# New durations in the planning clock of an S4D and MLP kernel, and outer products behind instead of ahead of x1

## The chip, the cores and the metric

The kernel runs on 1 core of a Trainium2 chip. The metric is the device time of one execution in microseconds, the median of several runs; less is better.

## What is computed

A layer norm of the input feeds two branches, and their product is added to the input. One branch is an S4D convolution: a kernel K made from exponentials of 128 modes for each of 576 channels, convolved with the sequence of 2048 steps by a Fourier transform. The other is an MLP with 4608 hidden units.

```
x  = A_u                                            # 1 x 2048 x 576
xn = layernorm(x)
P  = exp((A * dt)[:, :, None] * pos);  K = 2 * einsum("dn,dnl->dl", C, P).real
s  = irfft(rfft(xn_t, 2L) * rfft(K, 2L))[:L] + xn * D_skip
h  = gelu(layernorm(xn) @ w1 + b1);  g = silu(h @ w2 + b2)
out = x + s * g
```

## The kernel before

**The MLP.** All products are made with operands split into a high and a low part. The 2048 tokens are worked in two halves of 1024, each in two blocks of 512 (`tb`), and the 4608 hidden units in 12 groups of 384. One group with one block is a slot, 48 in all. A slot has 11 positions on TensorE: three of layer 1 (L617, 14 products of 512 columns each, into `mxa` and `mxb`) and eight of layer 2 (L680, products of 288 columns). For each product of layer 1 a chain follows it: Gelu on ScalarE (L653), its high part `hh` on ScalarE (L656), its low part `hl` on VectorE (L659); layer 2 needs `hh` and `hl`. After layer 2, VectorE adds the result to `acc` (L690). VectorE and ScalarE also split the raw weights (L567, L570).

**The scan.** The S4D branch is cut into 6 chunks of 96 channels, and its tables into 36 blocks of 16 channels. For each block, VectorE and ScalarE make tables of sines and magnitudes (L914 to L956), and TensorE makes K from them by outer products, `kgen` (L995). Each chunk then has on TensorE two steps x1 (L1099), two k1 (L1130), four s2 (L1160), two inverses (L1202) and one i1 (L1228). They write into two conversion banks, both called `cv`; VectorE or ScalarE empties them: transpositions after x1 and k1 (L1107, L1138), products and sums after s2 (L1175, L1181, L1182), transpositions between the two inverse stages (L1213). At the end the branches are combined (L727, L728), and the last rows are finished by L763 to L780. The row statistics of the later tokens (L407) are made during the first slots.

**The order.** Every engine's queue is written in the order in which a planner, `Order`, traces the steps. It keeps a virtual time for each engine. Each step carries an engine and a duration, which is what the text calls its booking; `dve(n)`, `act(n)` and `pool(n)` give durations from a number of columns. A step's results are ready after its booked duration and `LAT`, 0.2 us. TensorE's MLP positions are the backbone: `unit` takes them in turn, and `advance` then traces everything on other engines that can begin before TensorE's virtual time. The chains behind layer 1 and layer 2 are `urgent`, and each of their steps has a due time, `by`, worked out from TensorE's positions still to come (`hidden_by`, `add_by`). Other steps wait in `lines`; one is traced only if it ends before the due time of the next urgent step on its engine. TensorE's own scan steps are taken between MLP positions (`pe_turns`) if they were ready 0.4 us before, and x1, k1 and s2 are spread by a timetable (`pace`). `ride` lets a block of outer products join a host step x1, k1, s2 or i1: the block's function is put into `GUEST`, and the host calls `lead` with its own conversion bank. The start of the program, before the first slot, is written out by hand.

ScalarE keeps one table of functions at a time; `self.tbl` is the virtual clock's idea of it, and a change is booked at 1.28 us. Steps with `tbl=None`, copies and squares, run with any table.

Of the kernel before, what the change touches and what calls it, by code (L numbers as in the profile page):

```python
# [19 lines left out]
NT = 16  # L20
# [15 lines left out]
TB = 512  # L36
# [3 lines left out]
def dve(n):  # L40
    return 0.075 + 0.00104 * n


def act(n):
    return 0.06 + 0.00098 * n
# [6 lines left out]
class Order:  # L52
# [85 lines left out]
    def advance(self, horizon):  # L138
        while True:
            best = None  # L140
            soon = dict(self.next)
            for u in self.urgent:
                st = u[1][0]
                k = (max(u[0], self.t[st["eng"]]), 0)
                if u[0] <= horizon and (best is None or k < best[0]):
                    best = (k, u, None)
                for st in u[1]:
                    soon[st["eng"]] = min(soon.get(st["eng"], 1e9), st["by"])
            for x in self.lines:
                if x["steps"] and x["steps"][0]["by"] < 1e9:  # L150
                    st = x["steps"][0]
                    soon[st["eng"]] = min(soon.get(st["eng"], 1e9), max(st["by"], self.t[st["eng"]] + st["dur"]))
            for n, x in enumerate(self.lines):
                h = self.head(x)
                if h is None or h[0]["eng"] == "PE":
                    continue
                st, r = h
                if st["eng"] is None:
                    k = (max(r, 0), 1 + n)
                    if r > horizon:  # L160
                        continue
                else:
                    e = st["eng"]
                    b = max(self.t[e], r)
                    d = st["dur"]
                    if st["tbl"]:
                        d += 1.28 * (1 + (st["tbl"] != self.tbl))
                    if b > horizon or b + d > soon.get(e, 1e9) + st["late"]:
                        continue
                    k = (b, 1 + n)  # L170
                if best is None or k < best[0]:
                    best = (k, None, x)
            if best is None:
                break
            if best[1] is not None:
                self.go(best[1])
            else:
                self.run(best[2])
            self.pin()
# [26 lines left out]
def step(eng, dur, fn, need=(), mark=None, cv=0, at=0.0, late=0.0, tbl=None, by=1e9):  # L206
    return dict(eng=eng, dur=dur, fn=fn, need=tuple(need), mark=mark, cv=cv, at=at, late=late, tbl=tbl, by=by)
# [3 lines left out]
def mixer_kernel(ctx, tc, u, log_a_real, a_imag, c_real, c_imag, log_dt, d_skip, w1, b1, w2, b2,  # L211
                 f1, f2, g2, g1, tvals, ident, out, parts=("mlp", "s4d")):
    nc = tc.nc
# [145 lines left out]
    A2 = sb.tile([P, 16, 2, CH, 2], F32, name="A2")  # L359
# [617 lines left out]
    def lead(q):  # L977

        if GUEST:
            GUEST.pop()(q)  # L980
# [46 lines left out]
    def chunk(c):  # L1027
# [57 lines left out]
        def x1(i):  # L1085
            Q = {}
            in_parts("x", i, lambda: XC[i].rearrange("p b d -> p d b"), 32, [("xl", c, i)] + ([("x1", c, i - 1)] if i else []))

            def mm():
                a, b = PARTS2["x", i]  # L1090
                for v in range(2):
                    q = bank2("cv")
                    Q[24 * v] = q[:, :, :384].rearrange("p e (d b) -> p e d b", b=32)
                lead(q)
                for n, (f, x) in enumerate(((0, a), (0, b), (1, a))):
                    for e in range(2):
                        for v in range(2):
                            r = slice(64 * v, 64 * v + 64)
                            nc.tensor.matmul(Q[24 * v][:, e], FP[0][r, f, 0], x[r, 12 * e:12 * e + 12],  # L1099
                                             start=n == 0, stop=n == 2, skip_group_check=True)  # L1100
            add("PE", X1, mm, cv=2, mark=("x1", c, i), need=[("xp", c, i)])
            if i + 1 < CH // 48:
                four.append(step(None, 5.0, lambda: load(i + 1), mark=("xl", c, i + 1)))
            for d0 in (0, 24):
                for e in range(2):
                    c0 = 48 * i + d0 + 12 * e
                    add("DVE", 0.65, lambda d0=d0, e=e, c0=c0: nc.vector.transpose(  # L1107
                        A2[:, :, 0, c0:c0 + 12].rearrange("p k d r -> p d k r"), Q[d0][:, e]), cv=-e)

        def k1(i):  # L1110
            Q = {}
            k0 = c * CH // 4 + 12 * i

            def skip():
                nc.vector.tensor_add(KT[c, i][:, :, 0], KT[c, i][:, :, 0], dsk[:, k0:k0 + 12])
            kt = [("kt", b) for b in range(c * CH // SB + 3 * i, c * CH // SB + 3 * i + 3)]
            four.append(step("DVE", 0.2, skip, need=kt + ([] if c else [("pack", D // PK - 1), ("f2s", 7), "odd"] if i == 0 else [])))
            in_parts("k", i, lambda: KT[c, i], 64, [("k1", c, i - 1) if i else ("x1", c, CH // 48 - 1)])

            def mm():  # L1120
                a, b = PARTS2["k", i]
                for g0 in (0, 2):
                    q = bank2("cv")
                    Q[g0] = q[:, :, :384].rearrange("p g (d b) -> p g d b", b=32)
                lead(q)
                for n, (f, x) in enumerate(((0, a), (0, b), (1, a))):
                    for e in range(2):
                        for g in range(4):
                            r = slice(32 * g, 32 * g + 32)
                            nc.tensor.matmul(Q[g // 2 * 2][:, g % 2], FP[0][r, f, (e + g) % 2],  # L1130
                                             x[r, :, 32 * e:32 * e + 32], start=n == 0 and e == 0,
                                             stop=n == 2 and e == 1, skip_group_check=True)
                if i + 1 == CH // 48:
                    mats("f2t", 0)
                    od.marks["f2t", c] = od.t["PE"] + X1 + 5.0
            add("PE", X1, mm, cv=2, mark=("k1", c, i), need=[("kp", c, i)] + ([("i1", c - 1)] if c and i == 0 else []))
            for g in range(4):
                add("DVE", 0.65, lambda g=g: nc.vector.transpose(  # L1138
                    A2[:, :, 1, 48 * i + 12 * g:48 * i + 12 * g + 12].rearrange("p k d r -> p d k r"),
                    Q[g // 2 * 2][:, g % 2]),  # L1140
                    cv=-(g % 2))

        def s2(p):
# [27 lines left out]
            def prod(i):  # L1171

                PR[i] = sb.tile([P, 2, 4 * CH], F32, name="pr").rearrange("p t (a b d) -> p t a b d", a=2, b=2)
                for t in range(2):
                    nc.vector.tensor_mul(PR[i][:, t], bc(Q[i][:, t, 0::2], 2, 2), bc(KK[i][:, t], 1, 2))  # L1175
# [6 lines left out]
                nc.vector.tensor_add(y[:, i, 1], x[:, :, 0, 1], x[:, :, 1, 0])  # L1182
            for i in range(2):
                two.append(step("ACT", act(4 * CH), lambda i=i: copy(i), need=[("s2", c, p)]))
                two.append(step("DVE", 0.95, lambda i=i: prod(i), cv=-1))
                two.append(step("DVE", 0.63, lambda i=i: sums(i), mark=("sum", c, p) if i else None))
            if p % 2:
                inverse(p - 1)

# [20 lines left out]
                    A2[:, 4 * p + t:4 * p + t + 7:2, 0].rearrange("p i d r -> p r i d"), QI[t], AF.Copy), cv=-1))  # L1210

        def back(d0):
            add("DVE", 0.9, lambda: nc.vector.transpose(A2[:, :, 1, d0:d0 + 16].rearrange("p b d r -> p d b r"),  # L1213
                                                         A2[:, :, 0, d0:d0 + 16].rearrange("p k d r -> p d k r")))

        def i1():
# [290 lines left out]
    def end_line():  # L1507
        for c, c0, c1, sets in ((NCH - 3, 0, CE, [(b, 1) for b in range(8)]), (NCH - 1, CE, D, [(0, 3), (3, 3), (6, 2)])):
            for b, n in sets:
                a = (b, n, c0, c1)  # L1510
                ml["steps"].append(step(None, 10.0, lambda a=a: combine_load(*a), need=[("st", c), ("u", NT - 1)]))
                ml["steps"].append(step("DVE", 2 * dve(n * (c1 - c0)), lambda a=a: combine(*a)))
                ml["steps"].append(step(None, 4.0, lambda: None))


# [90 lines left out]
    for slot in range(NSLOT):  # L1606
# [5 lines left out]
        for pos in range(NPOS):  # L1612
            if pos < G:
# [17 lines left out]
                look_ahead(pos)  # L1631
                for k, (a, b, c) in enumerate(cell, pos + 1 - len(cell)):
                    by = hidden_by(pos, k)
                    od.urgent.append((od.t["PE"], [step("ACT", 0.62, a, tbl="gelu", by=by[0]),
                                                   step("ACT", act(TB), b, by=by[1]),
                                                   step("DVE", dve(TB), c, mark=("h", slot, k), by=by[2])]))
                od.advance(od.t["PE"])
                if pos == G - 1 and tb == 1 and slot + 1 < NSLOT:
# [96 lines left out]
```

## Time and profile before

| | |
|---|---|
| median of 3 runs | 1099.33 us (1098.7 to 1100.56) |
| profiled execution | 1101.59 us, its span 1099.8 us |
| TensorE clock granted in it | 0.999 |
| TensorE (PE) busy | 1089.1 us, 99% |
| VectorE (DVE) busy | 918.8 us, 84% |
| ScalarE (ACT) busy | 698.0 us, 63% |
| GpSimd (POOL) busy | 184.0 us, 17% |

A row of the groups reads: line, engine, operation, what it writes and reads, shapes, count, then busy time and the mean duration in ns, then the engine's idle time just before and what ended it. A row of the timeline reads: start, duration of the merged piece, engine, line, operation, count, and in brackets an idle time before it with what ended that. A row of the waits reads: who waited for whom, us in total, times, longest. PE's durations overlap, since matmuls are pipelined; the distance from one start to the next is what a matmul holds PE.

### The profile page before, as it was taken

The page shows a single profiled execution, that of the slowest core. Times are in us where ns is not written, and L with a number is a line of the kernel's source. Part 1 is how long each engine was busy: PE and PEld are TensorE (multiplying, and loading weights), DVE is VectorE, ACT ScalarE, POOL GpSimd, SP SyncE. Part 2 cuts the span into 40 slices and gives each one's busy share as a digit, 9 for nine tenths or more (in the row PEclk, how much of TensorE's full clock was granted, in tenths as well). Part 3 has the DMA queues.
Part 4 walks back from the last instruction along what each step waited for, and adds up shares of the span by engine and source line. Part 5 has one row for each costly group of instructions (what it writes and reads, how often), then busy time and mean ns, then how long its engine had stood idle before and what let it go on. Part 6 is the DMA issues. An engine that isn't in the chain of part 4 may idle for free.

```text
span 1099.8 us, 27208 instructions
## 1 busy us (share of the span) xinstructions
PE 1089.1 (99%) x11445; PEld 953.2 (87%) x11445; DVE 918.8 (84%) x1514; ACT 698.0 (63%) x1044; POOL 184.0 (17%) x255
## 2 busy tenths in 40 slices
PE   8999999999999999999999999999999999999997
PEld 7889989889888888888898888888888888888897
DVE  7698678979998899999999998898998986766356
ACT  6485699867667675676865857566775754324233
POOL 4557211161110100001100000000100012110220
PEclk9999999999999999999999999999999999999999
DMA  8836656735434252355623315242333426453453
GB/s 222 242 131 169 219 173 197 215 71 130 152 115 152 53 112 57 100 128 149 154 51 95 96 56 126 39 143 59 94 89 78 145 66 178 117 178 107 128 148 94
DMA packets 139651, 138.23 MB, mean 126 GB/s; under 512 B 88952, under 2 KB 105016, under 8 KB 138952
## 3 DMA queue, kind: packets, MB, share of 16 engines
q1 hardware_dynamic: 124664, 85.49, 29.6%
q0 software_dynamic: 14384, 50.27, 14.8%
q8 instruction: 89, 1.46, 0.6%
q10 hardware_dynamic: 480, 0.74, 0.3%
q14 instruction: 34, 0.28, 0.1%
HBM read 102.17 MB, written 36.63 MB: 126 GB/s over the span
## 4 chain that ended last, share of the span: by engine, by line
PE 95%; DMA 2%; SPq 2%; DVE 1%; issue 0%; ACTq 0%; ACT 0%; DVEq 0%
PE mxb L680 21%; PE mxa L680 21%; PE mxa L617 20%; PE mxb L617 20%; PE cv L995 3%; PE cv L1160 3%; PE cv L1202 2%; PE cv L1228 2%; PE cv L1130 1%; PE cv L1099 1%; SPq L808 1%; DMA w<-in_A_u_dram 1%; DMA acc<-in_A_u_dram 0%; DVE st L407 0%; DMA h<-in_B_b_dram 0%
## 5 line engine op out<-in xcount | busy, mean ns | idle before, releaser
L659 DVE TENSOR_TENSOR hl<-h,hh 128x512 fp32r<-128x512 f32 x144 | 98.8, 689 | 89.0 <-ACT hh L656 88.3
L680 PE MATMUL mxb<-w2h,hl 128*128 128x288 f32 x576 | 170.2, 295 | 1.8 <-DVE hl L659 1.8
L680 PE MATMUL mxb<-w2h,hh 128*128 128x288 f32 x576 | 171.6, 298 | 0.0
L680 PE MATMUL mxa<-w2h,hh 128*128 128x288 f32 x573 | 170.8, 298 | 0.0
L680 PE MATMUL mxb<-w2l,hh 128*128 128x288 f32 x576 | 169.5, 294 | 0.0
L680 PE MATMUL mxa<-w2h,hl 128*128 128x288 f32 x573 | 169.2, 295 | 0.0
L680 PE MATMUL mxa<-w2l,hh 128*128 128x288 f32 x573 | 168.6, 294 | 0.0
L653 ACT ACTIVATE h<-mxa,b1t 128x512 f32<-128x512 f32 x73 | 50.2, 689 | 110.9 <-PE mxa L617 109.9
L680 PEld LDWEIGHTS mxa<-w2h,hh 128*128 128x128 f32 x573 | 107.6, 188 | 6.6 <-issue 3.5
L680 PEld LDWEIGHTS mxb<-w2h,hh 128*128 128x128 f32 x576 | 108.1, 188 | 5.7 <-issue 1.8
L680 PEld LDWEIGHTS mxb<-w2h,hl 128*128 128x128 f32 x576 | 108.1, 188 | 2.3 <-DVE hl L659 2.3
L680 PEld LDWEIGHTS mxb<-w2l,hh 128*128 128x128 f32 x576 | 108.1, 188 | 0.6
L680 PEld LDWEIGHTS mxa<-w2l,hh 128*128 128x128 f32 x573 | 107.6, 188 | 0.7
L680 PEld LDWEIGHTS mxa<-w2h,hl 128*128 128x128 f32 x573 | 107.5, 188 | 0.1
L896 POOL DMA_DIRECT2D par<-par_s x36 | 27.8, 773 | 462.9 <-DVE mg L939 458.4
L656 ACT ACTIVATE hh<-h 128x512 fp32r<-128x512 f32 x144 | 90.6, 630 | 3.6
L653 ACT ACTIVATE h<-mxb,b1t 128x512 f32<-128x512 f32 x71 | 48.9, 689 | 68.8 <-PE mxb L617 66.4
L690 DVE TENSOR_TENSOR acc<-mxa,acc 128x576 f32<-128x576 f32 x87 | 65.5, 752 | 31.2 <-PE mxa L680 30.9
L617 PE MATMUL mxa<-XH,w1h 128*128 128x512 f32 x284 | 79.1, 400 | 0.0
L690 DVE TENSOR_TENSOR acc<-mxb,acc 128x576 f32<-128x576 f32 x88 | 66.1, 752 | 15.2 <-PE mxb L680 14.8
L617 PE MATMUL mxb<-XH,w1h 128*128 128x512 f32 x280 | 77.7, 399 | 0.0
L617 PE MATMUL mxa<-XL,w1h 128*128 128x512 f32 x284 | 76.1, 390 | 0.0
(269 smaller groups left out, 2483.8 us busy)
## 6 DMA issues: line engine op xcount, KB each, us to landing
raw<-in_B_w_dram SPq DMA_DIRECT2D x72, 288.0 KB, 3.4
raw<-in_B_w_dram SPq DMA_DIRECT2D x96, 192.0 KB, 3.8
par_s<-A POOLq DMA_DIRECT2D x4, 2160.0 KB, 8.2
par<-par_s POOLq DMA_DIRECT2D x36, 240.0 KB, 3.4
f2t<-f2q SPq DMA_DIRECT2D x24, 256.0 KB, 3.4
g2t<-g2p SPq DMA_DIRECT2D x24, 256.0 KB, 4.1
bias<-XR SPq DMA_DIRECT2D x42, 128.0 KB, 3.7
raw<-in_B_w_dram SPq DMA_DIRECT2D x48, 96.0 KB, 3.9
```

Source lines behind the costliest of these rows:

```text
L617: nc.tensor.matmul(q, a, b, start=j == 0 and i not in BEGUN, stop=j == len(ops) - 1, skip_group_check=True)
L653: nc.scalar.activation(t, q, AF.Gelu_apprx_tanh, bias=b1t[:, k:k + 1], scale=1.0)
L656: LAST[0] = nc.scalar.activation(hh[:, i], t, AF.Copy)
L659: nc.vector.tensor_sub(hl[:, i], t, hh[:, i].bitcast(F32))
L680: nc.tensor.matmul(q[:, dh, :288], a[:, i, c], b[:, i, d], start=i == 0 and k == 0 and not alone, stop=i == G - 1 and k == 2)
L690: nc.vector.tensor_add(o, q[:, dh:dh + n, :288], b)
L808: nc.sync.dma_start(r[32 * g:32 * g + 32].rearrange("c (b n) -> c b n", n=32), dram(src[k], 32 * g, [[N, 32], [32 * N, D // 32], [1, 32]]))
L896: nc.gpsimd.dma_start(PAR[b].rearrange("p (g i) k -> p g (i k)", g=4), dram(par_s, (b // 3 * 48 + b % 3 * 4) * NPAR, [[D * NPAR, P], [12 * ...
L995: nc.tensor.matmul(q[32 * g:32 * g + 32, i // 2, i % 2 * 64:i % 2 * 64 + 64], U[:, ri, 4 * g + i, :], v[:, ri, 4 * g + i, :], start=ri == ...
L1160: nc.tensor.matmul(Q[i][32 * q:32 * q + 32, f, 2 * ri:2 * ri + 2], m[r, 4 * i + q, 32 * ri:32 * ri + 32], A2[r, 4 * p + 2 * i + q // 2, :, ...
L1202: nc.tensor.matmul(QI[q // 2][64 * f:64 * f + 64, q % 2, i], MAT["g2t", p + i // 2][r, i % 2, f, ri], YS[p + i // 2][0][r, i % 2, ri, f], ...
L1228: nc.tensor.matmul(Q[h][64 * y:64 * y + 64, t], g1t.rearrange("p a e -> p (a e)"), A2[:, k:k + 2, 1].rearrange("p i d r -> p i r d"), star ...
```

## The change

Eight durations of the virtual clock are changed, one condition is added, and one call is moved.

- Transpositions after x1 and k1 0.65 to 0.48, between the inverse stages 0.90 to 0.64; the products after s2 0.95 to 1.01, the sums 0.63 to 0.56; a Gelu 0.62 to 0.67 and its high part from `act(512)`, 0.562, to 0.60; the load before a combining step 10 to 13, and the combining step 0.15 more.
- In `advance`, a ScalarE step without a table of its own is traced only if 1.28 us more are left before the next due time, when the table loaded is not Gelu's.
- In x1, `lead(q)` stands behind x1's products instead of ahead of them. A block that rides with x1 is issued after x1; k1, s2 and i1 keep theirs in front.

```
                     if st["tbl"]:
                         d += 1.28 * (1 + (st["tbl"] != self.tbl))
+                    elif e == "ACT" and self.tbl != "gelu":
+                        d += 1.28
                     if b > horizon or b + d > soon.get(e, 1e9) + st["late"]:
                         continue
...
-                lead(q)
                 for n, (f, x) in enumerate(((0, a), (0, b), (1, a))):
                     for e in range(2):
                         for v in range(2):
                             r = slice(64 * v, 64 * v + 64)
                             nc.tensor.matmul(Q[24 * v][:, e], FP[0][r, f, 0], x[r, 12 * e:12 * e + 12],
                                              start=n == 0, stop=n == 2, skip_group_check=True)
+                lead(q)
             add("PE", X1, mm, cv=2, mark=("x1", c, i), need=[("xp", c, i)])
...
-                    add("DVE", 0.65, lambda d0=d0, e=e, c0=c0: nc.vector.transpose(
+                    add("DVE", 0.48, lambda d0=d0, e=e, c0=c0: nc.vector.transpose(
...
-                add("DVE", 0.65, lambda g=g: nc.vector.transpose(
+                add("DVE", 0.48, lambda g=g: nc.vector.transpose(
...
-                two.append(step("DVE", 0.95, lambda i=i: prod(i), cv=-1))
-                two.append(step("DVE", 0.63, lambda i=i: sums(i), mark=("sum", c, p) if i else None))
+                two.append(step("DVE", 1.01, lambda i=i: prod(i), cv=-1))
+                two.append(step("DVE", 0.56, lambda i=i: sums(i), mark=("sum", c, p) if i else None))
...
-            add("DVE", 0.9, lambda: nc.vector.transpose(A2[:, :, 1, d0:d0 + 16].rearrange("p b d r -> p d b r"),
+            add("DVE", 0.64, lambda: nc.vector.transpose(A2[:, :, 1, d0:d0 + 16].rearrange("p b d r -> p d b r"),
...
-                ml["steps"].append(step(None, 10.0, lambda a=a: combine_load(*a), need=[("st", c), ("u", NT - 1)]))
-                ml["steps"].append(step("DVE", 2 * dve(n * (c1 - c0)), lambda a=a: combine(*a)))
+                ml["steps"].append(step(None, 13.0, lambda a=a: combine_load(*a), need=[("st", c), ("u", NT - 1)]))
+                ml["steps"].append(step("DVE", 2 * dve(n * (c1 - c0)) + 0.15, lambda a=a: combine(*a)))
...
-                    od.urgent.append((od.t["PE"], [step("ACT", 0.62, a, tbl="gelu", by=by[0]),
-                                                   step("ACT", act(TB), b, by=by[1]),
+                    od.urgent.append((od.t["PE"], [step("ACT", 0.67, a, tbl="gelu", by=by[0]),
+                                                   step("ACT", 0.6, b, by=by[1]),
```

## The prediction, made before the changed kernel ran

> **What bounds the kernel now.** I read the page first: the engine shares and the chain that ended last.
>
> ```profile
> PE 1089.1 (99%) x11445; PEld 953.2 (87%) x11445; DVE 918.8 (84%) x1514; ACT 698.0 (63%) x1044; POOL 184.0 (17%) x255
> PE 95%; DMA 2%; SPq 2%; DVE 1%; issue 0%; ACTq 0%; ACT 0%; DVEq 0%
> ```
>
> PE works in 99% of the span and is 95% of the chain. A share can hide stalls, since matmul ends are modelled, so I then asked the view of waits for PE alone. This is all it lists:
>
> ```profile
> PE mxb L680 <- DVE hl L659: 1.8, 2, 1.2
> PE mxa L1290 <- POOL XL L1283: 1.3, 1, 1.3
> PE cv L500 <- DVE row L440: 1.1, 1, 1.1
> PE mxa L632 <- ACT XH L504: 0.4, 1, 0.4
> ```
>
> 4.6 us of 1099.8, and none of it after the first 49 us: three of the four rows are the start, written out by hand and not touched by the change, and the fourth is two waits of the second slot. So the 1050 us in which the virtual clock orders the work run without one wait of PE. The change alters no product, no transfer and no byte; it alters the numbers by which the queues are ordered. What it can gain is the fourth row and the cost of switching PE between kinds of products; what it can lose is a wait that isn't there now.
>
> **The fourth row.** Here are the timeline of DVE and of PE in that slot.
>
> ```profile
> 43.78 0.82 DVE L407 BATCH_NORM_STATS2 st<-w 128x6 f32<-128x288 f32 x2 [3.77 <-DMA w<-in_A_u_dram]
> 45.32 0.67 DVE L659 TENSOR_TENSOR hl<-h,hh 128x512 fp32r<-128x512 f32 x1
> 44.56 0.30 PE L680 MATMUL mxb<-w2l,hh 128*128 128x288 f32 x1
> 46.05 0.40 PE L680 MATMUL mxb<-w2h,hl 128*128 128x288 f32 x1 [1.19 <-DVE hl L659]
> 48.01 0.29 PE L680 MATMUL mxb<-w2l,hh 128*128 128x288 f32 x1
> 48.93 0.40 PE L680 MATMUL mxb<-w2h,hl 128*128 128x288 f32 x1 [0.63 <-DVE hl L659]
> ```
>
> DVE sits 3.77 us in front of the row statistics (L407) until their rows of u land, and the low part that PE needs (hl, L659) stands behind them in the queue. The cause is the step of 6.0 us for that load, which the change leaves as it is. Of what it edits, only the Gelu and its high part run here. Each hl is booked 0.05 + 0.04 = 0.09 us later; the statistics are booked at 0.44 and 0.65 and stand in front of it because they were booked as ready before. A shift of 0.09 moves hl further behind them, not ahead. I therefore leave these waits in the sum: 0 us gained. (Issue to issue they cost PE 46.05 - 44.56 and 48.93 - 48.01 less 0.13 each, about 2.1 us; that is the most this place can give.)
>
> **The bookings on DVE.** Groups by line, then four timeline rows for what one really holds the engine, start to next start:
>
> ```profile
> L1107 DVE STREAM_TRANSPOSE A<-cv 128x384 f32<-128x384 f32 x48 | 24.4, 556 | 1.6 <-PE cv L1099 1.6
> L1213 DVE STREAM_TRANSPOSE A<-A 128x512 f32<-128x512 f32 x36 | 23.2, 686 | 1.8 <-ACT A L1209 1.8
> L1175 DVE TENSOR_TENSOR pr<-cv,kk 128x384 f32<-128x384 f32 x96 | 48.7, 549 | 2.0 <-ACT kk L1169 1.8
> 683.29 1.04 DVE L1107 STREAM_TRANSPOSE A<-cv 128x384 f32<-128x384 f32 x2
> 594.34 1.01 DVE L1175 TENSOR_TENSOR pr<-cv,kk 128x384 f32<-128x384 f32 x2
> 595.38 0.36 DVE L1181 TENSOR_TENSOR ys<-pr 128x192 f32<-128x192 f32 x1
> 595.93 0.69 DVE L952 TENSOR_TENSOR v<-w,mg 128x512 f32<-128x512 f32 x1
> ```
>
> Two transpositions take 1.04 with the second at 0.556, so one holds DVE 0.48; two products 595.38 - 594.34 = 1.04; two sums 595.93 - 595.38 = 0.55. The new bookings (0.48, 1.01, 0.56) fit these, the old ones (0.65, 0.95, 0.63) did not. In the virtual clock this is 96 x -0.17 (48 on L1107, as many on L1138) = -16.3, 36 x (0.64 - 0.90) = -9.4, 48 x 0.06 = +2.9 and 48 x -0.07 = -3.4: DVE is booked 26 us less over some 800 us. On the chip each of these instructions takes what it took. What goes is a hidden reserve of 4 x 0.17 = 0.7 us behind each of the 24 x1 and k1 steps. PE could start on a conversion bank too early only if that reserve held it back now; the list of PE's waits has neither L1107 nor L1138, and PE takes such a step only if it was booked ready 0.4 us before. Price 0; bounds, 0 to 24 x (0.7 - 0.4) = 7 us for a reserve that was used up everywhere, which I use in no case, since no row shows it used once.
>
> **The bookings on ACT.** Gelu 0.62 to 0.67, high part 0.562 to 0.60, 144 of each: 12.7 us more. And a copy that runs while another table than Gelu's is loaded is asked to leave 1.28 us for the load that follows.
>
> ```profile
> ACT h L653 <- PE mxa L617: 109.9, 54, 11.4
> ACT h L653 <- PE mxb L617: 66.4, 52, 2.6
> L653 ACT ACT_TABLE_LOAD x37 | 47.5, 1283 | 0.7
> 24.27 1.28 ACT L431 ACT_TABLE_LOAD   x1
> 25.56 0.30 ACT L431 ACTIVATE rs<-mv,tv 128x4 f32<-128x4 f32 x1
> ```
>
> In 106 of 144 Gelus ACT stands idle until PE has finished the product, 176 us together: ACT is early, not late, and PE's list has no wait on ACT behind the start. So a rule that keeps copies away from a Gelu guards against something that costs nothing now: price 0. It may push some copies and sines later, hidden by the same 176 us.
> The load's row says 1.28, and the next activation begins 1.29 after the load began. [...]
>
> **The tightest place.** The third Gelu of a slot has the least time; here in the last slot, one row each of ACT, ACT, DVE, PE:
>
> ```profile
> 1083.24 0.69 ACT L653 ACTIVATE h<-mxa,b1t 128x512 f32<-128x512 f32 x1 [1.82 <-PE mxa L617]
> 1083.96 0.63 ACT L656 ACTIVATE hh<-h 128x512 fp32r<-128x512 f32 x1
> 1084.63 0.69 DVE L659 TENSOR_TENSOR hl<-h,hh 128x512 fp32r<-128x512 f32 x1 [2.15 <-ACT hh L656]
> 1085.68 0.29 PE L680 MATMUL mxb<-w2h,hl 128*128 128x288 f32 x1
> ```
>
> hl ends at 1085.32 and is needed at 1085.68: 0.36 us. Slots without a scan product between layer 1 and that point look like this one; I count 18 of 48 in the trace (0.14 to 0.36 us), and this is the last of them. The change books the chain 0.09 longer, which pushes PE's virtual clock by less than 0.1 in such slots; DVE and ACT are in front of it as before. Price 0 as long as nothing is traced in front of hl.
>
> **Riding products.** 36 blocks of outer products (L995) run alone or in one group with another step. First a block alone, the first of 18; then one in front of its host, the last of 18; then the only one that rides with x1 (L1099).
>
> ```profile
> L995 PE MATMUL cv<-v,U 128*32 128x64 f32 x2304 | 39.6, 221 | 0.0
> 153.98 0.39 PE L617 MATMUL mxa<-XR,w1r 128*128 128x512 f32 x1
> 154.21 0.39 PE L617 MATMUL mxa<-XR,w1s 128*128 128x512 f32 x1
> 154.53 1.10 PE L995 MATMUL cv<-v,U 128*32 128x64 f32 x64
> 155.56 0.73 PE L617 MATMUL mxb<-XH,w1h 128*128 128x512 f32 x2
> 883.79 1.10 PE L995 MATMUL cv<-v,U 128*32 128x64 f32 x64
> 884.82 1.60 PE L1160 MATMUL cv<-A,f2t 64*32 64x192 f32 x64
> 394.10 1.10 PE L995 MATMUL cv<-v,U 128*32 128x64 f32 x64
> 395.13 0.62 PE L1099 MATMUL cv<-pr,f2t 64*128 64x384 f32 x4
> ```
>
> L617 goes out every 0.23, so L995 could start at 154.44 and starts at 154.53: 0.09. Behind it two L617 take 0.73 with the last at 0.39, 0.34 apart instead of 0.23: 0.11. Entering and leaving a group costs 0.2 us; the block itself takes 1.03 alone (155.56 - 154.53), with L1160 and with L1099 alike. A block that rides saves the 0.2. Putting it behind x1 instead of ahead changes neither count: 1.03 and the same group, price 0 for one block of 36, bounds -0.1 to +0.1 (the entry and the exit row). x1's four transpositions get their bank 1.03 us earlier there; nobody waits for them.
> What can change is how many ride, because DVE's work is booked 26 us shorter and the tables come ready earlier in the virtual clock, which gives a block longer to meet a host. Bounds: all 18 lone blocks find a host, -3.6 us; as many lose theirs, +3.6. I take two more, -0.4: the sign from the bookings, the size near nothing, for the pace of hosts is fixed by a timetable that isn't edited.
>
> **The end.**
>
> ```profile
> 1039.04 0.76 DVE L727 TENSOR_TENSOR row<-row 128x576 f32<-128x576 f32 x1 [2.70 <-DMA row<-g_s]
> 1075.47 0.55 DVE L727 TENSOR_TENSOR row<-row 128x384 f32<-128x384 f32 x1
> 1095.33 0.46 DVE L778 TENSOR_TENSOR v<-v,A 128x288 f32<-128x288 f32 x1
> ```
>
> The combining steps get 13 us for their loads instead of 10. The load at 1039 was 2.70 late, so the new number is nearer; the three last ones shift by 3 us each, 9 together, the last (L727 at 1075.47) to some 1085, ahead of the closing stretch that ends with L778 at 1095.79. If the scan finished over 3 us later, one would fall into that stretch and add its two operations, 1.1 us at most. Price 0.
>
> **Sum.** 0 (second slot) + 0 (DVE) + 0 (ACT) - 0.4 (rides) + 0 (end) = -0.4. Against the profiled execution's 1101.59 (span 1099.8): 1101.2, span 1099.4. The three timed runs have their median at 1099.33, 2.3 below that execution; on this scale 1098.9.
>
> **Rivals.** (1) Little moves, as summed: 1098.9; its own range is -2.1 (the second slot mends) to +1.6 (eight rides lost), 1097.2 to 1100.9. For it: no wait to remove, no queue late. That the re-booked clock gives the same order is part of it. Chance 0.70.
> (2) Faster: the second slot's statistics fall behind hl after all (-2.1) and half of the lone blocks ride (-1.8): 1095.4. Against it: the 6.0 us booking stays. Chance 0.13.
> (3) Slower: with DVE booked 26 us lighter, a table step is traced in front of an hl that it delays. One of 0.69 (L952 above) in front of an hl with 0.36 to spare costs PE 0.33 plus the 0.1 of a restart; it passes 0.2% (2.2 us) from six slots on, and if it happens in ten of the 18 tight ones, 4.3: 1103.6. For it: thin margins and a reserve taken away. Against it: each hl has a due time that steps have to respect, and that is not edited. Chance 0.16.
> [...] Chance 0.01. [...]
>
> **How the numbers follow.** 0.2% or 2.2 us is about what a measurement of this kernel can tell from no change. Faster 0.13 (case 2), within 0.70 (case 1), slower 0.17 (cases 3 and 4). The range takes case 1 whole and reaches half way into 2 and to three quarters of 3: 1096.3 to 1102.4, with about 0.15 outside.
>
> **What would show it.** Right: PE's list of waits has the same four rows, 1.8 us at L659 in the second slot among them; L1107 and L1138 last 556 ns; between 16 and 24 blocks of L995 ride. Wrong: new rows under PE's waits on hl, acc or a conversion bank; the row of L659 gone; DVE's wait before L407 shorter; the last L727 behind 1086.

## The result and the profile after

The changed kernel takes 1101.65 us, the median of 13 runs (1100.88 to 1103.33); the kernel before took 1099.16 in 13 runs beside it (1098.4 to 1101.46). The ratio is 1.0021 with an interval of 1.0013 to 1.0029: slower by 2.5 us. The profiled execution of after took 1101.89, its span is 1100.1.

The page's engine shares and its chain of after:

```profile
PE 1089.4 (99%) x11445; PEld 953.1 (87%) x11445; DVE 918.0 (83%) x1514; ACT 703.4 (64%) x1048; POOL 183.9 (17%) x255
PE 92%; DVE 3%; ACT 2%; DMA 1%; issue 1%; SPq 0%; ACTq 0%; DVEq 0%
```

PE's busy time is that of before to 0.3 us, so the shares tell nothing; the chain gives 3% to DVE and 2% to ACT, which had 1% and 0%. ACT has four instructions more, 1048 for 1044. PE's waits in after:

```profile
PE mxa L1292 <- POOL XL L1285: 1.3, 1, 1.3
PE mxb L682 <- DVE hl L661: 0.9, 2, 0.5
PE cv L502 <- DVE row L442: 0.8, 1, 0.8
PE mxa L682 <- DVE hl L661: 0.7, 1, 0.7
PE mxb L619 <- ACT h L655: 0.6, 1, 0.6
PE mxa L634 <- ACT XH L506: 0.4, 1, 0.4
```

Three rows hold waits behind the first 50 us, where before has none: the two on `hl` and the one on a Gelu. And here are PE's waits in a second profile of the kernel before (span 1097.7):

```profile
PE mxa L1290 <- POOL XL L1283: 1.3, 1, 1.3
PE mxa L632 <- ACT XH L504: 0.4, 1, 0.4
PE mxa L680 <- DVE hl L659: 0.2, 1, 0.2
```

The second slot's 1.8 us are not there. The profiled execution on which the prediction rests was one in which the load of `u` landed late, and so its span was 2.1 us longer. This comes and goes with the execution, whatever the order: 8 of the 19 profiles of this case lose 0.3 to 2.1 us of PE in that slot. The base for what follows is the second profile. In after, DVE waits 0.26 us in that slot instead of 3.77:

```profile
40.46 0.82 DVE L409 BATCH_NORM_STATS2 st<-w 128x6 f32<-128x288 f32 x2 [0.26 <-DMA w<-in_A_u_dram]
```

**First place, 258 us.** SyncE issuing a load, two ScalarE rows and one of PE in after, then the issue of the same load and ScalarE's step at L1075 (L1077 of after) in the second profile of before:

```profile
249.20 3.68 SPq L1042 DMA_DIRECT2D xc<-xn_s  x4
255.15 2.12 ACT L1077 ACTIVATE pr<-xc 128x768 fp32r<-128x768 f32 x1 [2.34 <-DMA xc<-xn_s]
257.29 1.28 ACT L655 ACT_TABLE_LOAD   x1
259.32 1.20 PE L619 MATMUL mxb<-XH,w1h 128*128 128x512 f32 x4 [0.57 <-ACT h L655]
...
236.62 2.47 SPq L1040 DMA_DIRECT2D xc<-xn_s  x4
246.19 2.09 ACT L1075 ACTIVATE pr<-xc 128x768 fp32r<-128x768 f32 x1
```

The four transfers of xc are booked at 5.0 us. Their issue alone took 3.68, and they had landed at 255.15, 5.95 after it began. ScalarE stood 2.34 us in front of L1077, and the table load (1.28 us) and the Gelu that come next in its queue were late for PE, which stood 0.57. The order of before had the load issued 9.6 us ahead of L1075 and reached it without a wait.

**Second place, 514 to 550 us,** where the first half of the tokens ends: a Tanh (L695, in after L697) runs there for each block, and rows of y are loaded for the second half. ScalarE, then DVE and PE in after, then ScalarE in the second profile of before:

```profile
513.20 1.17 ACT L933 ACTIVATE w<-w,tv 128x1040 f32<-128x1040 f32 x1
514.39 1.28 ACT L697 ACT_TABLE_LOAD   x1
517.12 1.28 ACT L655 ACT_TABLE_LOAD   x1
522.77 0.68 DVE L919 TENSOR_TENSOR w<-w,par 128x512 f32<-128x512 f32 x1
523.37 0.68 DVE L661 TENSOR_TENSOR hl<-h,hh 128x512 fp32r<-128x512 f32 x1
523.42 0.30 PE L682 MATMUL mxb<-w2l,hh 128*128 128x288 f32 x1
524.11 0.40 PE L682 MATMUL mxb<-w2h,hl 128*128 128x288 f32 x1 [0.39 <-DVE hl L661]
...
549.34 0.68 DVE L661 TENSOR_TENSOR hl<-h,hh 128x512 fp32r<-128x512 f32 x1
550.08 0.40 PE L682 MATMUL mxa<-w2h,hl 128*128 128x288 f32 x1 [0.70 <-DVE hl L661]
...
510.49 1.07 ACT L926 ACTIVATE w<-w 128x1040 f32<-128x1040 f32 x1 [1.01 <-DVE w L923]
511.47 0.76 ACT L695 ACTIVATE h<-acc 128x288 f32<-128x288 f32 x2
```

In after the Tanh comes behind a sine step and loads a table of its own, and the Gelu behind it loads once more. The virtual clock books a Tanh as one of Gelu's table, so the second load of 1.28 us is not in it. It happens at 514 and at 536. In before L695 has none (16 Tanhs, 0 loads); L697 of after has 2 for 16. ScalarE runs late from there, `hl` behind it as well: PE loses 0.56, 0.69, 0.19 and 0.86 us between 523 and 550.

**The account.** From one start to the next PE usually takes 0.13 us at L682 and 0.23 at L619. I add up what is beyond that, where it is 0.125 or more, behind the start that is written by hand: 3.16 us in after (0.73 at 258, 0.13 at 481, 0.56, 0.69, 0.19, 0.86; 3.86 in its second profile), 0.34 in before. The opening stretch, up to the first L682, took 0.6 longer in this execution. 23 blocks ride instead of 18, which at the prediction's 0.2 each is -1.0. Sum 2.82 + 0.6 - 1.0 = 2.4; PE's last matmul came 2.45 later. The closing stretch behind it is the same, 6.4 us.

### The profile page after: what moved, and what is told of

It reads as the page before. It is cut to its first block, busy times and chain, and to the rows that moved or that the text cites. A ratio compares the mean times of both kernels' runs of the same rounds, so it can differ in the third digit from the quotient of the medians.

```text
span 1100.1 us, 27212 instructions
## 1 busy us (share of the span) xinstructions
PE 1089.4 (99%) x11445; PEld 953.1 (87%) x11445; DVE 918.0 (83%) x1514; ACT 703.4 (64%) x1048; POOL 183.9 (17%) x255
## 3 DMA queue, kind: packets, MB, share of 16 engines
q8 instruction: 89, 1.46, 0.5%
## 4 chain that ended last, share of the span: by engine, by line
PE 92%; DVE 3%; ACT 2%; DMA 1%; issue 1%; SPq 0%; ACTq 0%; DVEq 0%
PE mxb L682 20%; PE mxa L682 20%; PE mxa L619 20%; PE mxb L619 19%; PE cv L1162 3%; PE cv L997 3%; PE cv L1204 2%; PE cv L1132 1%; PE cv L1230 1%; PE cv L1100 1%; DVE acc L692 1%; DMA acc<-in_A_u_dram 0%; DVE XL L487 0%; PE mxa L634 0%; DVE ys L1081 0%
## 5 line engine op out<-in xcount | busy, mean ns | idle before, releaser
L682 PE MATMUL mxb<-w2h,hh 128*128 128x288 f32 x576 | 171.3, 297 | 0.0
L682 PE MATMUL mxb<-w2h,hl 128*128 128x288 f32 x576 | 170.3, 296 | 0.9 <-DVE hl L661 0.9
L682 PE MATMUL mxa<-w2h,hh 128*128 128x288 f32 x573 | 170.6, 298 | 0.0
L682 PE MATMUL mxa<-w2h,hl 128*128 128x288 f32 x573 | 169.3, 295 | 0.7 <-DVE hl L661 0.7
L682 PE MATMUL mxb<-w2l,hh 128*128 128x288 f32 x576 | 169.5, 294 | 0.0
L682 PE MATMUL mxa<-w2l,hh 128*128 128x288 f32 x573 | 168.6, 294 | 0.0
L655 ACT ACTIVATE h<-mxa,b1t 128x512 f32<-128x512 f32 x73 | 50.1, 687 | 113.3 <-PE mxa L619 111.8
L682 PEld LDWEIGHTS mxa<-w2h,hh 128*128 128x128 f32 x573 | 107.6, 188 | 6.3 <-issue 4.2
L682 PEld LDWEIGHTS mxb<-w2h,hh 128*128 128x128 f32 x576 | 108.2, 188 | 5.6 <-issue 2.4
L682 PEld LDWEIGHTS mxb<-w2h,hl 128*128 128x128 f32 x576 | 108.1, 188 | 1.6 <-DVE hl L661 1.6
L682 PEld LDWEIGHTS mxb<-w2l,hh 128*128 128x128 f32 x576 | 108.2, 188 | 0.6
L682 PEld LDWEIGHTS mxa<-w2h,hl 128*128 128x128 f32 x573 | 107.5, 188 | 1.2 <-DVE hl L661 1.2
L682 PEld LDWEIGHTS mxa<-w2l,hh 128*128 128x128 f32 x573 | 107.6, 188 | 0.7
L655 ACT ACTIVATE h<-mxb,b1t 128x512 f32<-128x512 f32 x71 | 48.9, 688 | 68.4 <-PE mxb L619 62.0
L619 PE MATMUL mxa<-XH,w1h 128*128 128x512 f32 x284 | 79.2, 401 | 0.0
L619 PE MATMUL mxb<-XH,w1h 128*128 128x512 f32 x280 | 77.9, 400 | 0.6 <-ACT h L655 0.6
L619 PE MATMUL mxa<-XL,w1h 128*128 128x512 f32 x284 | 76.1, 390 | 0.0
```

The lines of the kernel that those rows point to most:

```text
L619: nc.tensor.matmul(q, a, b, start=j == 0 and i not in BEGUN, stop=j == len(ops) - 1, skip_group_check=True)
L655: nc.scalar.activation(t, q, AF.Gelu_apprx_tanh, bias=b1t[:, k:k + 1], scale=1.0)
L682: nc.tensor.matmul(q[:, dh, :288], a[:, i, c], b[:, i, d], start=i == 0 and k == 0 and not alone, stop=i == G - 1 and k == 2)
```

## The experiments

Line numbers are those of before in kernels built on it, those of after (2 more from L168 on) in the others; the one-column Gelu of the table edit adds 2 more. All ratios are to the kernel before, run beside.

**Both kernels again.**

> The kernel before, unchanged, profiled a second time. Its first profiled execution took 1101.59 us, 2.4 above its median of 1099.16, and holds two waits of PE on hl in the second slot, 2.1 us together. Theory A (those waits came with that one execution, because the load of u landed late in it): this profile shows no wait of PE behind the start over 0.3 us, a span of 1097.5 +- 0.5. Theory B (they stand in every execution): the same two waits, span 1099.5 to 1100, and the changed kernel's loss is not in waits. Ratio to the kernel before 1.000 in both.

> The changed kernel, unchanged, profiled a second time. Theory A: its five waits of PE (0.7 at 258 us, 0.6 and 0.7 at 523 and 526, 0.2 and 0.9 at 547 and 549, 3.1 us together) come from the order of the queues and stand in this profile too, at the same places within 0.3 us each; ratio 1.0021 +- 0.0008. Theory B (waits differ from execution to execution, the loss lies in how groups are put together): other places, sum under 1.5 us, same ratio.

Before: 1099.67, ratio 1.0001 (0.9992 to 1.001). After: 1102.19, ratio 1.0028 (1.0018 to 1.0038), with its waits at the same places. The difference holds.

**Half of the bookings each.** e1_gelu is the kernel before with this alone:

```
-                    od.urgent.append((od.t["PE"], [step("ACT", 0.62, a, tbl="gelu", by=by[0]),
-                                                   step("ACT", act(TB), b, by=by[1]),
+                    od.urgent.append((od.t["PE"], [step("ACT", 0.67, a, tbl="gelu", by=by[0]),
+                                                   step("ACT", 0.6, b, by=by[1]),
```

e1_dve is the kernel before with the five VectorE bookings of x1, k1, s2 and the inverse's turn alone.

> The kernel before with only the bookings of Gelu (0.67) and its high part (0.60). 15 of 36 outer product blocks ride instead of 18, which by 0.2 us each is +0.6. Theory A with the Gelu bookings as the cause of the waits: 2 to 3 us of waits on hl or on a Gelu, 1.002 to 1.003. With the DVE bookings as the cause: no new waits, 1.0005 (the three rides).

> The kernel before with only the bookings on DVE (transpositions 0.48 and 0.64, products 1.01, sums 0.56). 20 blocks ride, -0.4. With the DVE bookings as the cause of the waits: 2 to 3 us of waits on hl, 1.0015 to 1.0025. With the Gelu bookings as the cause: no new waits, 0.9995.

e1_gelu: 1107.88, ratio 1.0081 (1.0068 to 1.0093), the dearest of all. e1_dve: 1102.5, ratio 1.0027 (1.0016 to 1.0038). Neither half is free, and neither is the cause by itself. In e1_gelu the largest wait stands behind another load, the rows of y, booked at 6.5 us. DVE, then PE, then two-microsecond windows, which give the busy time of PE, PE's weight loads, DVE, ACT and POOL with their instructions, PE's granted clock (third from last: 0.96, 0.50, 0.84), the share of the DMA engines and GB/s:

```profile
482.09 0.71 DVE L475 STREAM_TRANSPOSE row<-row 128x512 f32<-128x512 f32 x1 [2.84 <-DMA row<-y_s]
483.71 0.71 DVE L475 STREAM_TRANSPOSE row<-row 128x512 f32<-128x512 f32 x1 [0.91 <-DMA row<-y_s]
484.35 0.65 DVE L659 TENSOR_TENSOR hl<-h,hh 128x512 fp32r<-128x512 f32 x1
485.06 0.61 PE L680 MATMUL mxb<-w2h,hl 128*128 128x288 f32 x1 [3.26 <-DVE hl L659]
...
482.00:484.00 2.00, 0.00 (x0) 0.00 (x0) 1.00 (x2) 1.98 (x4) 0.00 (x0) 0.96 0.37 54
484.00:486.00 2.00, 0.94 (x4) 0.95 (x5) 2.00 (x5) 1.99 (x3) 0.00 (x0) 0.50 0.79 126
490.00:492.00 2.00, 2.00 (x14) 2.00 (x14) 1.62 (x5) 0.00 (x0) 0.00 (x0) 0.84 0.75 145
```

The wait of 3.26 us costs twice: the clock is granted at half from 483.8, inside the wait, to 490.6, 5.6 us of it under work. PE's products start 0.24 us apart there instead of 0.13, which costs another 2.4. In e1_dve the waits are others again: 0.9 us at 289 behind the load of f2t (booked 5.0) and 0.96 at 521 behind the Tanh's and the Gelu's tables.

**The table mended, in the order of after.** e2_after_table adds to after, ahead of the Tanh:

```
+            if od.tbl != "gelu":
+                nc.scalar.activation(small[:, 5:6], epst[:, 0:1], AF.Gelu_apprx_tanh)
```

e2_after_tq is that with two of the four transfers of each later xc load of the first chunk on ScalarE's queue.

> The changed kernel, its order of steps untouched, with one Gelu of a single column issued ahead of a Tanh of the gate where the virtual clock's table is not Gelu's. Tanh and Gelu are booked as one table; in the changed kernel's profile two Tanhs that follow sines bring a table of their own (L697, 2 loads of 1.28 us) and the next Gelu loads again. Theory A1 (these two unbooked loads make ScalarE late between 515 and 550 us, and so the waits at 523, 526, 547 and 549, 2.3 us): L697 has no table load any more, the four waits fall to under 0.5 us together, ratio 1.0028 - 0.0020 = 1.0008 +- 0.0006. Theory A2 (VectorE, booked too light, is late there by itself): the loads go, the waits stay, ratio 1.0025 to 1.003.

> As the one before, and of the four transfers that load the second half of chunk 0 (xc) two go out on ScalarE's queue instead of SyncE's; the order of steps is again untouched. Theory A3 (the wait at 258 us, 0.7 to 1.1 us, is a load booked at 5.0 us that needs 5.9, because four transfers are issued one after the other at 0.92 us): the wait falls below 0.3, ratio 0.0006 to 0.0009 below the kernel before this one, so 1.0000 +- 0.0006. Else (ScalarE is late there for its own work): the wait stays or grows by the two issues, no lower ratio.

e2_after_table: 1105.12, ratio 1.005 (1.0038 to 1.0062), some 3 us worse than after. The loads at L697 are gone, and so are the waits at 523 and 549; that at 526 fell from 0.69 to 0.26. But the wait at 545 grew from 0.19 to 3.06:

```profile
539.62 1.85 SPq L472 DMA_DIRECT2D row<-y_s  x2
546.87 0.70 DVE L477 STREAM_TRANSPOSE row<-row 64x512 f32<-64x512 f32 x1 [4.06 <-DMA row<-y_s]
548.67 0.40 PE L682 MATMUL mxa<-w2h,hl 128*128 128x288 f32 x1 [2.90 <-DVE hl L661]
...
550.00:552.00 2.00, 2.00 (x11) 2.00 (x10) 2.00 (x4) 1.48 (x1) 0.00 (x0) 0.50 0.00 0
```

DVE now reached the turning of the y rows early, and the rows landed 7.25 us after their issue began; that issue had stood on SyncE behind 3.7 us of xc. Again the half clock followed (3.4 us, in which 1.5 were lost). e2_after_tq: 1104.47, ratio 1.0048 (1.0034 to 1.0063); the wait at 258 was 1.46, no smaller. Moving half of xc to ScalarE's queue didn't help.

**Longer bookings for the loads.** e2_gelu_loads is e1_gelu with 6.5 for xc and 9.0 for the y rows; e2_after_all is e2_after_table with these and 7.0 for f2t.

> The kernel with the Gelu bookings alone (1.0081, waits of PE of 1.5 at 258, 0.7 at 360 and 3.7 at 481 to 485 us), with two loads booked longer: xc 6.5 instead of 5.0, the rows of y 9.0 instead of 6.5. The planner's order changes with it. Theory A3 (queues blocked by a load that was booked too short make its large waits): no wait of PE behind an xc or y row reader, those of 258 and 481 gone, 19 blocks ride, ratio 1.001 to 1.003. Else (the longer Gelu booking itself spoils the order): the waits come back elsewhere at the same size, 1.006 or more.

> The changed kernel with the table repair and with all the loads seen late booked longer (xc 6.5, rows of y 9.0, f2t 7.0); order new, 18 blocks ride as in the kernel before. If the waits come from misbooked loads and tables alone: no wait of PE over 0.3 us behind the start, 1.000 +- 0.0007. If each new order brings waits of its own, whatever is booked: 1.002 or more.

e2_gelu_loads: 1102.42, ratio 1.0032 (1.002 to 1.0044): the waits of 258 and 481 are gone, two new ones stand at 568 and 571 (0.75 and 1.24), and the kernel is 5.5 us faster than e1_gelu. In front of both new ones DVE works without a gap, and no load is late. e2_after_all: 1102.73, ratio 1.0033 (1.0021 to 1.0045): one large wait is left, 1.74 us at 573, where DVE works without a gap and no load is late, and only 18 blocks ride. Its closing stretch is 1.2 us longer than that of before, 1.1 of it a combining step ahead of DVE's last steps. A longer booking makes yet another order.

**Other pieces of the change.** e3_no_gelu is after without Gelu's and the high part's bookings; e3_tr and e3_back are the kernel before with only the transpositions' 0.48, and only the inverse's 0.64; e3_dve_table is e1_dve with the one-column Gelu.

> The kernel after, with the bookings of Gelu and high part as before (0.62 and 0.556); all other edits stay. It makes an order of its own (22 rides). Theory A (every new order comes upon some of the loads and table switches that the virtual clock books too short, whichever booking made it): 1100.5 to 1103.5, with one to three waits of TensorE over 0.5 us at places other than those of the kernel before, each behind a load or the Tanh. Theory B (the waits belong to Gelu's bookings, the rest is harmless): 1098.4 to 1099.5, no new row under TensorE's waits. Theory C (the virtual clock's own end, 1105.9 against 1107.4 for the kernel before, tells it): 1098.0.

> The kernel before with one booking alone changed: the transpositions of x1 and k1 at 0.48 for 0.65. An order of its own again (17 rides). Theory A: 1100 to 1103, waits at new places. Theory D (what the VectorE bookings together cost, 3 us, is the transpositions' doing): about 1102.4, and the next kernel at the time before. Theory C: virtual end 1107.3 against 1107.4, so 1099.4.

> The kernel before with the booking of the 128x768 turn at L1213 alone changed, 0.64 for 0.9 (18 rides). Theory A: 1100 to 1103, waits at new places. Theory D: 1099.4, since the transpositions keep their booking. Theory C: virtual end 1109.1 against 1107.4, so 1101.2.

> All VectorE bookings of the change on the kernel before, as in e1_dve, and a Gelu over one column ahead of the Tanh where the table is not Gelu's: the order on every queue is that of e1_dve. If the table load at L695 is what TensorE waited 0.96 us for at 520.8 us in e1_dve, that wait goes and the time is about 1101.5, unless the y rows' load or another step is next late at the same place, as it was when the same column went into the kernel after: then 1102 to 1104 with a wait on hl between 515 and 552 us. The 0.9 us at 289 us behind the load of f2t stays in both cases.

e3_no_gelu: 1105.27, ratio 1.0046 (1.0033 to 1.0059). e3_tr: 1106.11, 1.0057 (1.0044 to 1.0069). e3_back: 1102.59, 1.0025 (1.0016 to 1.0034). e3_dve_table: 1101.94, 1.0019 (1.001 to 1.0028). One booking of one kind of step, e3_tr's, costs 6.3 us, more than the whole change; the parts do not add up, since each makes its own order. The virtual clock's end is no guide either: its best order of these, e3_no_gelu (a virtual end of 1105.9 against 1107.4 for before), was 5.5 us above before. In e3_no_gelu a wait of 1.05 us stands at 887 behind no load at all; DVE has six table steps and two combining ones in a row in front of `hl` there, which is the mechanism of the prediction's third rival. Its closing stretch is 1.4 us longer, 1.1 of it a combining step ahead of DVE's last steps; that is the risk, and the price, which the prediction's step on the end had named. In e3_dve_table the wait at 521 is gone, as expected.

**The late loads on another queue, in the order of after.** e4_rows_pool is e2_after_table with the y rows on GpSimd's queue, e4_pool also with half of xc there:

```
-                nc.sync.dma_start(T[0][32 * g:32 * g + 32]...
+                nc.gpsimd.dma_start(T[0][32 * g:32 * g + 32]...
...
-                    nc.sync.dma_start(XC[i][64 * v + 32 * e:...
+                    (nc.gpsimd if v and i and not c else nc.sync).dma_start(XC[i][64 * v + 32 * e:...
```

> The kernel e2_after_table (after, with a Gelu over one column ahead of a Tanh that finds another table) with the loads of the y rows issued on GpSimd's queue instead of SyncE's; every engine's order is that of after. Theory late loads: in e2_after_table the two transfers of the last y rows stood on SyncE behind 3.7 us of xc transfers, landed at 546.87, and VectorE waited 4.06 us for them in front of hl. Issued on GpSimd they land some 3 us earlier; the 3.06 us wait at 545 us and the 1.7 us lost at half clock behind it go: 1105.1 less 4 to 4.8, 1100.3 to 1101. Theory next one late: the place keeps a wait of over 1 us (behind GpSimd's stores of g, which stand in the same queue, or another step): 1102 to 1105.

> The same, and two of the four transfers of each later xc load of the first chunk on GpSimd's queue too. Theory late loads: xc at 255 us lands 1 to 2 us earlier, the wait of 1.2 us at 258 goes as well, and what is left of the order of after is its five more rides (1.0 us): 1098.7 to 1099.7, level with or below the kernel before. Theory next one late: 1101 or more, with a wait of over 0.5 us at 258 or elsewhere.

e4_rows_pool: 1101.51, ratio 1.0017 (1.0008 to 1.0025); e4_pool: 1098.55, ratio 0.9992 (0.9981 to 1.0002). The order on PE, DVE and ScalarE is that of after, to the last step, with the two one-column Gelus added. GpSimd, DVE, SyncE and ScalarE in e4_pool, then two rows of PE's waits:

```profile
533.73 0.68 POOL L472 DMA_DIRECT2D row<-y_s  x1
542.35 0.70 DVE L477 STREAM_TRANSPOSE row<-row 64x512 f32<-64x512 f32 x1
249.54 1.38 SPq L1044 DMA_DIRECT2D xc<-xn_s  x2
254.67 2.12 ACT L1079 ACTIVATE pr<-xc 128x768 fp32r<-128x768 f32 x1 [1.51 <-DMA xc<-xn_s]
...
PE mxb L682 <- DVE hl L661: 0.6, 1, 0.6
PE mxb L619 <- ACT h L655: 0.2, 1, 0.2
```

The issue of the y rows begins 5.9 us sooner and DVE doesn't wait for them; the wait on xc is 1.51 instead of 2.34, which the Gelu behind it can bear. The 0.6 is the load of the second slot, at 46 us, late in this execution; the 0.2 is a Gelu at 682 us.

**What the mended order is worth.** e5_before_pool has the same three edits on the kernel before, whose order stays (no Tanh meets another table there, so the one-column Gelu is never issued); e5_after_pool_no_table is e4_pool without the one-column Gelu; e5_pool_again is e4_pool.

> The kernel before with the three edits of e4_pool (one-column Gelu ahead of a Tanh that finds another table, y rows and half of the xc transfers of the first chunk on GpSimd's queue); its order stays that of before. Theory late loads: nothing that these edits mend is late in the order of before (TensorE's waits after the start are 0.2 us in its second profile), so 1099.0 to 1100, level with before; then what e4_pool has over it is the order that the change makes, five more rides at 0.2 us. Rival: the edits are a gain in any order, and this one falls by 1 us or more, to 1098.5 or less.

> e4_pool without the one-column Gelu: the order of after, late loads mended, the two table loads of the Tanh at 514 and 536 us left in. Theory: the Tanh's loads carry the waits of 0.56, 0.69 and 0.86 us at 523, 526 and 549 us, about 2 us with the 0.2 at 546; they stay, so 1098.6 + 1.8 (0.26 of them stands in e4_pool too) = 1100.4, bounds 1100 to 1101. Rival: those waits were the y rows' as well, and the time is that of e4_pool, 1098.6.

> e4_pool once more, beside the two others: 1098 to 1099.2; 1 us below before if the five more rides are all that sets it apart, level with before if the 1098.55 was luck of the executions.

e5_before_pool: 1101.02, ratio 1.001 (1.0001 to 1.0019). e5_after_pool_no_table: 1100.84, 1.0005 (0.9996 to 1.0014). e5_pool_again: 1098.54, 0.9992 (0.9983 to 1.0). Without the table edit the waits at 523 to 550 are back (0.57, 0.69, 0.19, 0.86). Two rows of PE's waits in e5_after_pool_no_table, then the row on `hl` in e5_pool_again, which is the second slot's alone:

```profile
PE mxb L682 <- DVE hl L661: 1.1, 3, 0.5
PE mxa L682 <- DVE hl L661: 0.7, 1, 0.7
...
PE mxb L682 <- DVE hl L661: 0.7, 1, 0.7
```

With all three edits the order of after is the fastest of the kernels tried, 0.08% below before with an interval that touches 1. That doesn't yet make it the better order, because the end of the span differs too. Here is the last step of DVE in e4_pool (span 1096.9), then in e5_before_pool (span 1098.6):

```profile
1093.00 0.46 DVE L782 TENSOR_TENSOR v<-v,A 128x288 f32<-128x288 f32 x1
...
1093.07 0.46 DVE L780 TENSOR_TENSOR v<-v,A 128x288 f32<-128x288 f32 x1
```

Up to here the two are level. Behind it, where the last stores of the result land, e4_pool, e5_pool_again and e5_after_pool_no_table take 3.4 us, before and after 4.0, e5_before_pool 5.0 and e4_rows_pool 5.1. So 1.6 of the 2.5 us between e5_before_pool and e4_pool, and 0.6 of the 1.2 between before and e4_pool, lie behind all work of PE and DVE. What sets it no run shows. On PE's work alone the three edits are no gain in the order of before (its last matmul starts 0.1 sooner), and the mended order of after is level with before within 0.2 us, with 0.7 and 0.9 us of the second slot's late load in its two profiles.

The account of most runs against the second profile of before, in us: PE's extra distances after the start, those between one line and the next among them; time inside or behind them that they don't show (half clock, and stops in a riding group, the last section); the sum with 0.2 a ride and with the opening stretch, which varied by 0 to 1.2; and what PE's last matmul came later by. The closing stretch is not in it.

| kernel | ride | waits | other | sum | measured |
|---|---|---|---|---|---|
| before, second profile | 18 | 0.34 | | | |
| after | 23 | 3.16 | | 2.4 | 2.45 |
| e1_gelu | 15 | 6.70 | 2.4 | 9.4 | 9.5 |
| e1_dve | 20 | 2.16 | 1.1 | 2.7 | 2.8 |
| e2_after_table | 23 | 4.69 | 1.5 | 4.8 | 4.4 |
| e2_after_all | 18 | 2.09 | | 2.7 | 2.3 |
| e3_no_gelu | 22 | 4.37 | 1.7 | 4.9 | 4.4 |
| e3_tr | 17 | 3.65 | 1.6 | 5.3 | 5.9 |
| e3_back | 18 | 2.96 | 0.3 | 3.4 | 4.2 |
| e3_dve_table | 20 | 0.44 | 2.0 | 2.3 | 2.5 |
| e4_pool | 23 | 1.50 | | 0.2 | -0.2 |

It closes within 0.8 us in each: up to PE's last matmul, what an order costs are its waits, and what it gains are its rides. The 0.2 a ride is an estimate from the prediction's rows; no run changed the rides alone.

## Why the prediction was wrong

The forecast was 1098.9, little moved, at 0.70. The time is 1101.65, just outside that case's own range (up to 1100.9) and inside the range given. That the range holds it is luck: it reached so far up for rival 3, not for late loads and table loads. Step by step:

- **The second slot, 0.** Misread. Its row was taken for a standing wait; it belongs to that execution. The 2.3 us between the profiled execution and the median should have told it. The scale to the median made up for it, so the sum lost nothing, but rivals 1 and 2 count on a gain of 2.1 that the median has already.
- **VectorE's bookings, 0: failed.** e1_dve, e3_tr and e3_back put them at 2.8 to 6.3 us, each alone. The step asked whether PE would start a product too early on a conversion bank, which no trace shows. The step didn't ask what else moves when DVE's virtual time is shorter by 26 us: the whole order on DVE and ScalarE is dealt anew. Steps that wait for a load are reached before it lands, and in some orders DVE's own steps stand without a gap in front of `hl`. The loads' bookings (5.0 for xc that took 5.95, 6.5 for y rows that took 7.25) were not edited and so not looked at.
- **ScalarE's bookings, 0: failed**, most of all (8.4 us alone). The 176 us in which ScalarE is idle before a Gelu is a sum over the span; it doesn't cover the one Gelu in front of which a load or two table loads stand. The new condition was rightly 0: traced with that edit alone, the kernel before keeps every queue's order. The table load's 1.28 was right too, the number of loads was not: 84 became 88, two of them at the Tanh. No run shows a term for case 4 (chance 0.01): in after the 38 loads of Gelu's table at L655 last 1283 ns each, and the Gelu behind the one at 257.29 begins 1.29 us after it.
- **The tightest place.** With 0.36 us or less to spare in such a slot, a late step reaches PE; the margin was read rightly, and "as long as nothing is traced in front of hl" was the condition that didn't hold.
- **Rides, -0.4:** right in sign, too small: five more, not two, and the account closes with about 0.2 each.
- **`lead` behind x1, the end, 0:** near enough. The one group of x1 with its rider takes 2.5 us with its entry instead of 2.7 in before, twice the bound. The last combining step (L729 of after) ran at 1073, where the second profile of before has it, not at 1085, and the closing stretch didn't change. No run tried either edit alone.
- **What would show it.** L1107 and L1138 last 550 and 554 ns and 23 blocks ride, as foretold; the new rows on `hl`, the missing row of the second slot and the short wait before L407 are those it named as proof against it.
- **Rival 3** had the sign but not the mechanism: not many tight slots by 0.43 each, but two places by about 3 us in all, one started by a load that the virtual clock books too short, the other by table loads that it doesn't book. Its mechanism does show in other orders: in front of the waits of e2_gelu_loads at 568 and 571, e2_after_all at 573 and e3_no_gelu at 887.

One thing stays open. That the old, too long bookings had kept steps clear of these loads by a margin is a reading; no run shows it apart from the chance that the order of before simply happened to miss them.

## What to carry to other kernels

Where a planner writes the queues, a better number for one step is a new order for all: look for the steps in that planner whose numbers are too small (loads by issue to landing, table switches), not only for those that were edited. One late load made late work of what stood behind it in the queue (ScalarE idle for 2.34 us in front of L1077, PE for 0.57 behind the Gelu that followed), so price the wait by who stands behind. Idle time summed over a kernel says nothing of the place where the margin is 0.4 us.

## What the chip showed that was not expected

- **Two long waits cost twice.** With the wait of 3.26 us the clock fell to half for 6.8 us (e1_gelu, from 483.8 to 490.6), with that of 2.90 for 3.4 us (e2_after_table, from 549.3, 0.6 us behind the wait's end). None of the waits of up to 1.7 us did that (the mean granted clock is 0.999 in e2_after_all, which has its 1.74), nor the 2.0 of the next point (1.00 from 320 to 324). What sets the length no run shows.
- **PE stopped inside a group with nothing late in the kernel.** In e3_dve_table, PE and the packets of the instruction queue in the window 321 to 322 (packets, MB, share of the DMA engines):

```profile
320.55 1.55 PE L1162 MATMUL cv<-A,f2t 64*32 64x192 f32 x50
323.60 0.57 PE L1162 MATMUL cv<-A,f2t 64*32 64x192 f32 x14 [1.49 <-issue]
...
q8 instruction: 1, 0.02, 5.5%
```

  A block of outer products and s2 issue 128 matmuls, with as many weight loads, in 2.6 us. PE stopped after the 50th of s2's 64, which cost 2.0 us (the product behind the group starts 3.55 us after the group's first, in before 1.54 at 884.82); one 16 KB packet of instructions came in that window (the profile has 89, 1.46 MB in all), and PE went on some 1.4 us after it ended. e1_dve, e3_tr and e3_no_gelu stop at the same 50th, for 1.0 to 1.7 us, and go on 1.2 to 1.4 us after such a packet. No run tested whether the packet is the cause of the stop.
- **A Tanh behind a sine** loaded a table of its own in after (L697 at 514.39 and 535.94, 1.28 us each), and the next Gelu loaded again (517.12 and 538.94, 1.28 each); the other Tanhs of after, and all 16 of before, brought no load, among them the one at 519.00, right behind a Gelu.
